# An FFT and maxout kernel on one core: stage one of the later batches in two groups of three, the single row by itself, and four edits at the two ends

## The chip, the core and the metric

The kernel runs on one core of a Trainium2 chip. A core has five engines with instruction streams of their own: TensorE (PE) multiplies matrices, with the loading of weights shown apart (PEld); VectorE (DVE), ScalarE (ACT) and GpSimd (POOL) do elementwise work; SyncE (SP) issues DMA transfers, as POOL and ACT can too. Engines wait for each other through semaphores. The metric is the device time of one execution in microseconds. Of the kernel before, the median of 3 runs is 388.24 us (387.73 to 388.91).

## The reference

```python
X = np.fft.fft(x, axis=1)            # x: (8, 3072, 256) float32
X = np.fft.fft(X, axis=2)
x = X.real.reshape(24576, 256)
h = np.maximum(np.maximum(x @ w1, x @ w2), x @ w3)   # w1, w2, w3: 256 x 768
out = h @ w_out                      # w_out: 768 x 256, out (24576, 256) float32
```

The Fourier transform runs over the sequence and over the channels, of which the real part is kept. Each of the 24576 rows then goes through three products, of which the largest is kept element by element, and an output layer.

## The kernel before

The transforms are matrix products with tables of cosines and sines. Over the sequence they are done in two stages. **Stage one** (`Mix.s`, from L386) multiplies the rows of one batch, held in `xt` as 49 rows of 256 columns with a mirrored copy in the lower half of the partitions, by a table `tab` of 64 columns. `s(0)` to `s(5)` take eight rows each with two matmuls side by side: `tile_position` (0, 0) and (0, 64) put the two products into the two halves of a PSUM bank. `s(6)` takes the single row 48, 64 output partitions by 128 columns (L404). ACT (in batch 1 DVE for some) copies each bank to `tb`. The result is transposed: in batch 0 on DVE, in later batches by a trip through DRAM, out with `y(0)`, `y(1)` and back with `z(0)`, `z(1)`, all issued by SP. **Stage two** (`Mix.k`) multiplies by the long tables and yields `tE` and `tO`, an even and an odd part over the first 1536 positions of the sequence. Even plus odd gives a row, even minus odd its mirrored row, so that half of the positions suffice.

The FFN of one batch is cut into 18 **units**: 3 blocks of 512 tokens by 6 chunks of 128 of the 768 hidden columns. The channel transform is folded into the weights (`g_all`, `gd_all`). Every unit yields `hp` for the plus rows and `hm` for the mirrored ones, and comes in two kinds:

- unsplit: `unit_plus` with four full matmuls (128x128 weights, 512 columns), ACT's `stmp` (L497) and DVE's maximum (L498) for `hp`; then `unit_minus` with two more matmuls, `stmp` and maximum again for `hm`. Six matmuls.
- split: `third(g)` computes the third product's even and odd part (two matmuls, L856 and L858), which ACT (`odd`, L860) and DVE (`even`, L861) bring to SBUF and POOL adds and subtracts (`plus` and `minus`, L865). `begin(g)` adds two matmuls (L875, L876) and one DVE operation (L877, `hp`), `finish(g)` one matmul (L491) and one DVE operation (L889, `hm`). Five matmuls, and two operations of POOL.

All odd units from unit 7 of batch 0 on are split; of the even ones those that `EXTRA` and `EXTRA_LAST` list: none in batch 0, units 0, 4, 8, 12 and 14 in the others. The output layer (`l2_block` and `l2_last`, matmuls L547, L563, L570) of each block is spread over the units of the next one.

The order on every engine is written out by hand: nothing is rearranged by a scheduler. The main loop walks over all 8 x 18 units: it begins unit g, finishes the unit before (where that one is split and g is not, it is finished first), computes the third product of unit g+2, issues scattering stores of mirrored rows at some units, then up to ten steps of the output layer, and then what `plan` holds for this unit: pieces of the next batch's stages (`ahead0` for batch 1, `ahead` for batches 2 to 7), loads of x (`load_x`, at units 13 and 18 of three batches before), and the mirror copies (`turn` and `mirror_first`). These copies are on ACT in eight parts, from units 5 to 12 of the batch two ahead of the one that they serve (3 units later for batch 2). 

PSUM banks: `ps_f` has three, shared in turn by stage one and two, the third products' `e3` and `d3`, and `pl`; `ps_s`, `ps_l1`, `ps_w3` and `ps_o` hold the head's products, the units' and the output layer's. In `ahead`, stage one of a later batch is in units 1 to 3: `s0`, `s1`; `s2`, `y0`, `s3`, `s6`; `s4`, `s5`, `y1`, `u` (`u` copies column 0 for a correction).

The head runs before the main loop: loads, the tables, batch 0's mirror copies in four parts (`FIRST`), stage one of batch 0 with some warming-up matmuls between, the transpose on DVE (L427), `k_first` for stage two of the first block (L696, evicted to `tE` and `tO` at L698), and the folded weights (L311 to L341, `gd_all` at L332). The mirror copies of batch 0 take column 0 separately (L133): on ACT, and on POOL for the parts from row 40 on.

Of the kernel before, what the change touches and what calls it, by code (L numbers as in the profile page):

```python
# [9 lines left out]
FP32 = mybir.dt.float32  # L10
# [4 lines left out]
ALU = mybir.AluOpType  # L15
# [13 lines left out]

FIRST_OF = (4, 8, 1)  # L30
PACE = (0, 4, 8, 14)
EXTRA, EXTRA_LAST = (0, 4, 8, 12, 14), (0, 4, 8, 12, 14)


def _parts(g):

    done = [(12 + i - 1, slice(128 * i + 96, 128 * i + 128)) for i in range(4)]
    for i in range(4 if g < 2 else 3):
        done.append((FIRST_OF[g] + i - 1, slice(128 * i, 128 * i + 96)))
    if g == 2:  # L40
        done += [(16, slice(384, 480, 2)), (15, slice(385, 480, 2))]
    return done
# [3 lines left out]
def kernel(  # L46
# [9 lines left out]
    nc = tc.nc  # L56

    B, S, D = x.shape
# [3 lines left out]
    TOKB = 512  # L62
    NHALF = 1536
    UNITS = 3 * NJC
# [8 lines left out]
    ps_f = ctx.enter_context(tc.tile_pool(name="ps_f", bufs=3, space=bass.MemoryType.PSUM))  # L73
# [30 lines left out]
    g_all = consts.tile([128, 4 * DFF], BF16, tag="g_all")  # L104
    g_all = g_all.rearrange("p (c k j) -> p c k j", k=4, j=128)
# [6 lines left out]
    sgn = consts.tile([128, 1], FP32, tag="sgn")  # L112
    wcol = consts.tile([128, NJC], FP32, tag="wcol")
    dif = consts.tile([128, 1], FP32, tag="dif")
# [9 lines left out]
    def mirror(b, s0, s1):  # L124

        t = xt[b % 2]
        fn = (nc.vector.tensor_copy, (nc.gpsimd.tensor_copy, nc.vector.tensor_copy)[s0 >= 25],
              nc.scalar.copy)[min(b, 2)]
        fn(out=t[64:128, s0:s1, 1:128], in_=t[0:64, s0:s1, 255:128:-1])  # L129
        if b < 2:  # L130
            if b == 0:
                fn = nc.scalar.copy if s0 < 40 else nc.gpsimd.tensor_copy
            fn(out=t[64:128, s0:s1, 0], in_=t[0:64, s0:s1, 128])  # L133

    def mirror_first(b):

        t = xt[b % 2]
        nc.scalar.copy(out=t[64:128, :, 0], in_=t[0:64, :, 128])
# [3 lines left out]
    ps_s = ps_s_cm.__enter__()  # L142
# [7 lines left out]
    pidx = gen.tile([128, 1], FP32, tag="pidx")  # L150
# [56 lines left out]
    turn = gen.tile([128, 2], FP32, tag="turn")  # L207
# [127 lines left out]
    def prep_first():  # L335

        for i in range(2):
            for half in range(2):
                psg = ps_f.tile([128, 512], FP32, name="psg", tag="ps")
                product(psg, 0, i, half, 384, 768)  # L340
                (nc.vector.tensor_copy, nc.scalar.copy)[half](  # L341
                    out=g_all[:, 3:6, 2 * i + half, :],
                    in_=psg[:, 0:384].rearrange("p (c j) -> p c j", j=128))
                if half:
                    differ(i, i + 1, 384, 768)
                yield
# [34 lines left out]
    class Mix:  # L381
# [8 lines left out]
        def s(self, k, pool=ps_f, evict=nc.scalar.copy):  # L390
            ps1 = pool.tile([128, 512], FP32, name="ps1", tag="ps")
            if k < 6:
                for hh in range(2):
                    nc.tensor.matmul(ps1[hh * 64:hh * 64 + 64], tab,  # L394
                                     self.x[:, 8 * k + hh:8 * k + 8:2, 0:128],
                                     start=True, stop=True, tile_position=(0, 64 * hh))
                if self.b:
                    evict(out=tbv[:, 4 * k:4 * k + 4, :],
                          in_=ps1.rearrange("p (s f) -> p s f", s=4))
                else:  # L400
                    evict(out=tbt[:, :, 4 * k:4 * k + 4, :],
                          in_=ps1.rearrange("p (s f l) -> p f s l", s=4, l=2))
            else:
                nc.tensor.matmul(ps1[0:64, 0:128], tab, self.x[:, 48, 0:128],  # L404
                                 start=True, stop=True, tile_position=(0, 0))
                if self.b:
                    evict(out=tbv[0:64, 24, :], in_=ps1[0:64, 0:128])
                else:
                    evict(out=tbt[0:64, :, 24, :],
                          in_=ps1[0:64, 0:128].rearrange("p (f l) -> p f l", l=2))  # L410
# [65 lines left out]
                                 tab[:, NHALF:NHALF + 1], start=True, stop=True)  # L476
            nc.scalar.copy(out=t_mid[:, :, self.b], in_=ps3[:, 0:2])

    def unit_plus(te, to, jc, n, pool3, tag3):

        pse2 = ps_l1.tile([128, TOKB], FP32, name="pse2", tag="pse2")
        pse3 = pool3.tile([128, TOKB], FP32, name="pse3", tag=tag3)
        for (pse, i) in ((pse2, 0), (pse3, 1)):
            nc.tensor.matmul(pse[:, 0:n], g_all[:, jc, 2 * i, :], te, start=True, stop=False)  # L484
            nc.tensor.matmul(pse[:, 0:n], g_all[:, jc, 2 * i + 1, :], to, start=False, stop=True)  # L485
        return pse2, pse3

    def unit_minus(pses, to, jc):
# [177 lines left out]
    def warm_up(n):  # L666
        for _ in range(n):
            nc.tensor.matmul(warm, zero[:, 0:128], zero, start=True, stop=True)
# [10 lines left out]
    m.s(2, pool=ps_s)  # L679
    m.s(3, pool=ps_s)  # L680
    warm_up(1)
    mirror(0, *FIRST[3])
    m.s(4, pool=ps_s)
    warm_up(2)
# [4 lines left out]
    def k_first(which):  # L689

        for h in range(2):
            ps2 = ps_s.tile([128, 512], FP32, name="ps2", tag="ps")
            for (i, cols) in _parts(0):
                at = cols.start - 256 * h
                if 0 <= at < 256:
                    nc.tensor.matmul(ps2[:, at:at + cols.stop - cols.start], m.col(i, which),  # L696
                                     (te_tab, to_tab)[which][:, cols], start=True, stop=True)
            (dve, nc.scalar.copy)[h](out=(m.tE, m.tO)[which][:, 256 * h:256 * h + 256],  # L698
                                     in_=ps2[:, 0:256])

    m.s(6, pool=ps_s)
    m.t()
    scal(sgn, pidx, 0.0, ALU.is_equal)
    scal(sgn, sgn, 2.0, ALU.mult, -1.0, ALU.add)
    scal(dif, sgn, 1.0, ALU.subtract)
    warm_up(2)
    nc.scalar.activation(out=nmd_all, in_=vm, func=AX.Sin, scale=float(-2.0 * math.pi / 256.0),
                         bias=turn[:, 1:2])
# [46 lines left out]
    ps_w3 = ctx.enter_context(tc.tile_pool(name="ps_w3", bufs=1, space=bass.MemoryType.PSUM))  # L755
    ps_o = ctx.enter_context(tc.tile_pool(name="ps_o", bufs=2, space=bass.MemoryType.PSUM))
# [3 lines left out]
    first, second = prep_first(), prep_second()  # L760
# [10 lines left out]
    def at(b, unit, fn):  # L771
        plan.setdefault((b + unit // UNITS, unit % UNITS), []).append(fn)
# [27 lines left out]
    def turn(b, ch):  # L800
        mirror(b, *EIGHTHS[ch])
# [16 lines left out]
    for b in range(2, B):  # L818
        for h in range(2):
            if b > 2:  # L820
                at(b - 3, (13, 18)[h], lambda b=b, h=h: load_x(b, 0, NS, h))
        for ch in range(8):
            at(b - 2, 5 + ch + 3 * (b == 2), lambda b=b, ch=ch: turn(b, ch))
        at(b - 2, 13 + 3 * (b == 2), lambda b=b: mirror_first(b))

    ahead0 = {3: ("s0", "s1"), 4: ("s2", "y0"), 5: ("s3", "s4"), 6: ("s5", "s6", "y1", "u"),
              7: ("z0", "z1"), 12: ("x",), 13: ("kO0",), 14: ("v0", "kE0", "kO1"),
              15: ("v1", "kE1"), 16: ("kO2",), 17: ("v2", "kE2", "end")}
    ahead = {1: ("s0", "s1"), 2: ("s2", "y0", "s3", "s6"), 3: ("s4", "s5", "y1", "u"),
             5: ("z0", "z1"), 11: ("x",), 12: ("kO0",), 13: ("v0", "kE0", "kO1"),  # L830
             14: ("v1", "kE1"), 15: ("kO2",), 16: ("v2", "kE2", "end")}
    for b in range(B - 1):
# [5 lines left out]

    def is_split(g):
        if g % 2 == 0:  # L840
            return (UNITS <= g < B * UNITS and
                    g % UNITS in (EXTRA if g < (B - 1) * UNITS else EXTRA_LAST))
        return 7 <= g < B * UNITS

    def operands(g):
# [21 lines left out]
    def begin(g, dst):  # L867

        te, to, _, jc = operands(g)
        if is_split(g):  # L870
            if g % 2:
                pse2 = ps_l1.tile([128, TOKB], FP32, name="pse2", tag="pse2")
            else:
                pse2 = ps_w3.tile([128, TOKB], FP32, name="pse3", tag="pse3")
            nc.tensor.matmul(pse2, g_all[:, jc, 0, :], te, start=True, stop=False)  # L875
            nc.tensor.matmul(pse2, g_all[:, jc, 1, :], to, start=False, stop=True)  # L876
            nc.vector.scalar_tensor_tensor(out=dst, in0=pse2, scalar=0.0, in1=sums[g][0],  # L877
                                           op0=ALU.max, op1=ALU.max)
            return (pse2,)
        pses = unit_plus(te, to, jc, TOKB, *((ps_o, "po") if g % 2 else (ps_w3, "pse3")))  # L880
        unit_out(pses, dst, TOKB)
        return pses

# [11 lines left out]
    for g in range(B * UNITS):  # L895
        b, u = divmod(g, UNITS)
        blk, jc = divmod(u, NJC)
# [68 lines left out]
```

## Time and profile before

| | |
|---|---|
| median of 3 runs | 388.24 us |
| profiled execution | 388.26 us |
| its span, first to last instruction | 386.5 us |
| granted TensorE clock | 1.00 |
| PE busy | 369.5 us, 96% |
| DVE, POOL, ACT busy | 87%, 86%, 63% |

Rows of the timeline give the start in microseconds from the start of the span, the duration (of several alike, from the first start to the last end), the engine, the line of the code (L12), the operation, output and inputs by the program's names with their sizes, the count (x2), and in brackets the idle time of the engine just before and what ended it. For a matmul the weights' shape comes first: 128*128 is a full one, 128*64 one that uses half of the array's columns. Matmuls overlap, so what one costs is read from one start to the next; their ends are modelled, and some of their records are missing from the trace. Rows of the windows give the window, its length, and the busy time (and count) of PE, PEld, DVE, ACT and POOL, the granted clock, the DMA engines' share and GB/s. Lines of the page are busy time, share and count of each engine.

### The profile page before, as it was taken

What the parts mean: (1) busy time and instruction counts of PE and PEld (TensorE: products, weight loads), DVE (VectorE), ACT (ScalarE), POOL (GpSimd) and SP (SyncE); (2) the same over time, 40 slices, a digit from 0 to 9 for tenths busy, and PEclk for the clock granted to TensorE, in tenths of its full rate; (3) what the DMA queues carried; (4) which work ended last, traced back from release to release, by engine and by line L of the source; (5) the groups of instructions that cost most, each with busy time, mean ns of one, the idle gap of its engine ahead of it and who ended that gap; (6) DMA issues with size and microseconds to landing.
All of it is one profiled execution on the core that took longest, in us unless ns stands there. A gap on an engine that the chain in (4) does not pass through costs nothing.

```text
span 386.5 us, 7957 instructions
## 1 busy us (share of the span) xinstructions
PE 369.5 (96%) x2737; PEld 234.8 (61%) x2786; DVE 335.7 (87%) x566; ACT 242.7 (63%) x455; POOL 331.7 (86%) x355
## 2 busy tenths in 40 slices
PE   6699999999999999999999999999999999999994
PEld 2354566565665666656665666666665667666664
DVE  7798797789997998989987998989987998989982
ACT  6877789567756677567756777567856436434320
POOL 9994557968999899989999899989988899879991
PEclk9999999999999999999999999999999999999999
DMA  8999736695269735695269834695224633312217
GB/s 118 168 197 152 158 114 101 189 162 177 71 133 204 196 120 106 181 213 180 67 120 200 209 110 112 188 187 184 85 56 128 186 113 97 96 61 98 77 63 225
DMA packets 51299, 54.13 MB, mean 140 GB/s; under 512 B 25813, under 2 KB 44268, under 8 KB 50563
## 3 DMA queue, kind: packets, MB, share of 16 engines
q0 software_dynamic: 19392, 26.45, 33.3%
q1 hardware_dynamic: 31334, 26.57, 26.5%
q10 hardware_dynamic: 532, 0.59, 0.5%
q8 instruction: 22, 0.36, 0.4%
q14 instruction: 19, 0.16, 0.1%
HBM read 36.95 MB, written 30.81 MB: 175 GB/s over the span
## 4 chain that ended last, share of the span: by engine, by line
PE 81%; POOL 9%; DVE 4%; issue 3%; ACT 2%; DVEq 0%; POOLq 0%
PE po L547 29%; PE pse L491 9%; PE pse L876 5%; PE e L856 5%; PE d L858 5%; PE pse L875 5%; PE po L570 4%; PE pse L485 4%; PE pse L484 3%; PE ps L460 3%; POOL plus L865 3%; PE ps L394 3%; PE pl L563 2%; POOL minus L865 2%; POOL xt L122 1%
## 5 line engine op out<-in xcount | busy, mean ns | idle before, releaser
L865 POOL TENSOR_TENSOR plus<-even,odd 128x512 bf16<-128x512 f32 x104 | 132.0, 1269 | 38.5 <-DVE even L861 31.1
L865 POOL TENSOR_TENSOR minus<-even,odd 128x512 bf16<-128x512 f32 x104 | 132.1, 1270 | 0.0
L860 ACT ACTIVATE odd<-d 128x512 f32<-128x512 f32 x104 | 62.1, 597 | 63.8 <-PE d L858 50.3
L877 DVE SCALAR_TENSOR_TENSOR hp<-pse,plus 128x512 bf16<-128x512 f32 x104 | 71.4, 687 | 26.0 <-PE pse L876 21.5
L547 PE MATMUL po<-wout_bf,hp 128*128 128x256 bf16 x576 | 86.1, 273 | 0.0
L547 PE MATMUL po<-wout_bf,hm 128*128 128x256 bf16 x576 | 78.6, 273 | 0.0
L861 DVE SCALAR_TENSOR_TENSOR even<-vb,wcol,e 128x512 f32<-128x512 bf16 x104 | 76.6, 737 | 0.0
L547 PEld LDWEIGHTS <-hp 128*128 128x128 bf16 x576 | 56.3, 98 | 26.2
L889 DVE SCALAR_TENSOR_TENSOR hm<-pse,minus 128x512 bf16<-128x512 f32 x104 | 70.7, 680 | 0.8 <-PE pse L485 0.4
L547 PEld LDWEIGHTS <-hm 128*128 128x128 bf16 x576 | 56.3, 98 | 16.3
L491 PE MATMUL pse<-tO,gd_all 128*128 128x512 bf16 x183 | 63.2, 380 | 0.8 <-DVE hp L877 0.2
L497 ACT ACTIVATE stmp<-pse 128x512 bf16<-128x512 f32 x80 | 47.5, 599 | 19.0 <-PE pse L491 8.8
L129 ACT COPY xt<-xt 64x762 bf16<-64x762 bf16 (+1 forms) x48 | 39.8, 838 | 2.3 <-DMA xt<-in_x_dram 1.3
L575 DVE TENSOR_TENSOR kq<-po,even 128x512 f32<-128x512 f32 x60 | 40.9, 682 | 0.0
L856 PE MATMUL e<-tE,g_all 128*128 128x512 bf16 x104 | 39.4, 379 | 0.3
L858 PE MATMUL d<-tO,gd_all 128*128 128x512 bf16 x104 | 39.4, 379 | 0.0
L876 PE MATMUL pse<-tO,g_all 128*128 128x512 bf16 x94 | 35.6, 379 | 1.7 <-issue 1.0
L570 PE MATMUL po<-gw,tO 128*128 128x512 bf16 x92 | 34.9, 379 | 0.0
L498 DVE TENSOR_TENSOR hp<-pse,stmp 128x512 bf16<-128x512 f32 x40 | 27.5, 687 | 6.7 <-ACT stmp L497 3.6
L875 PE MATMUL pse<-tE,g_all 128*128 128x512 bf16 x84 | 31.9, 380 | 0.7 <-DVE hm L498 0.5
L567 ACT COPY even<-pl 128x512 f32<-128x512 f32 x46 | 26.8, 583 | 8.3 <-DVE kq L575 7.8
L498 DVE TENSOR_TENSOR hm<-pse,stmp 128x512 bf16<-128x512 f32 x40 | 27.5, 687 | 4.2 <-ACT stmp L497 3.0
(183 smaller groups left out, 485.4 us busy)
## 6 DMA issues: line engine op xcount, KB each, us to landing
db<-tb SPq DMA_DIRECT2D x21, 192.0 KB
xt<-in_x_dram POOLq DMA_DIRECT2D x5, 784.0 KB, 8.2
xt<-in_x_dram POOLq DMA_DIRECT2D x5, 752.0 KB, 8.7
out_dram<-obuf SPq DMA_DIRECT2D x8, 384.0 KB
out_dram<-kq SPq DMA_DIRECT2D x8, 384.0 KB
vb<-vd SPq DMA_DIRECT2D x23, 128.0 KB
out_dram<-kq SPq DMA_DIRECT2D x7, 288.0 KB
out_dram<-kq SPq DMA_DIRECT2D x15, 128.0 KB
```

What stands on the lines that cost most here:

```text
L491: nc.tensor.matmul(pse, gd_all[:, jc, i, :], to, start=False, stop=True, skip_group_check=True)
L498: nc.vector.tensor_tensor(out=dst, in0=src3, in1=stmp[:, 0:n], op=ALU.max)
L547: nc.tensor.matmul(po, hcols(jc), wout_bf[:, jc * 256:(jc + 1) * 256], start=False, stop=(jc == NJC - 1), skip_group_check=True)
L856: nc.tensor.matmul(e3, g_all[:, jc, 2, :], te, start=True, stop=True)
L858: nc.tensor.matmul(d3, gd_all[:, jc, 1, :], to, start=True, stop=True)
L860: nc.scalar.activation(out=odd3, in_=d3, func=AX.Copy, scale=-0.5)
L861: nc.vector.scalar_tensor_tensor(out=even3, in0=vb, scalar=wcol[:, jc:jc + 1], in1=e3, op0=ALU.mult, op1=ALU.add)
L865: nc.gpsimd.tensor_tensor(out=dst, in0=even3, in1=odd3, op=op)
L875: nc.tensor.matmul(pse2, g_all[:, jc, 0, :], te, start=True, stop=False)
L876: nc.tensor.matmul(pse2, g_all[:, jc, 1, :], to, start=False, stop=True)
L877: nc.vector.scalar_tensor_tensor(out=dst, in0=pse2, scalar=0.0, in1=sums[g][0], op0=ALU.max, op1=ALU.max)
L889: nc.vector.scalar_tensor_tensor(out=dst, in0=pses[0], scalar=0.0, in1=sums.pop(g)[1], op0=ALU.max, op1=ALU.max)
```

## The change

Five things change.

1. In `ahead`, the pieces of stage one of batches 2 to 7 stand in units 1 to 3 as `s0`, `s1`, `s2`, `y0`; `s3`, `s4`, `s5`; `s6`, `y1`, `u`. The matmul of the single row loses its `tile_position`.
2. Units 12 and 14 of batch 0 are split, and unit 14 of the last batch is not.
3. Batch 3's mirror copies, `turn` and `mirror_first`, come one unit later.
4. In the head, column 0 of the parts from row 40 on is copied by DVE; the three one-column operations on `sgn` and `dif` move ahead of a mirror copy; `k_first(1)` takes its banks from `ps_f`.
5. Unit 0 runs its four matmuls as even, even, odd, odd.

```diff
-EXTRA, EXTRA_LAST = (0, 4, 8, 12, 14), (0, 4, 8, 12, 14)
+EXTRA = (12, 14), (0, 4, 8, 12, 14), (0, 4, 8, 12)
...
             if b == 0:
-                fn = nc.scalar.copy if s0 < 40 else nc.gpsimd.tensor_copy
+                fn = nc.scalar.copy if s0 < 40 else nc.vector.tensor_copy
             fn(out=t[64:128, s0:s1, 0], in_=t[0:64, s0:s1, 128])
...
                 nc.tensor.matmul(ps1[0:64, 0:128], tab, self.x[:, 48, 0:128],
-                                 start=True, stop=True, tile_position=(0, 0))
+                                 start=True, stop=True)
...
-        for (pse, i) in ((pse2, 0), (pse3, 1)):
-            nc.tensor.matmul(pse[:, 0:n], g_all[:, jc, 2 * i, :], te, start=True, stop=False)
-            nc.tensor.matmul(pse[:, 0:n], g_all[:, jc, 2 * i + 1, :], to, start=False, stop=True)
+        steps = [(pse2, 0, 0), (pse2, 0, 1), (pse3, 1, 0), (pse3, 1, 1)]
+        if first:
+            steps = steps[0::2] + steps[1::2]
+        for (pse, i, k) in steps:
+            nc.tensor.matmul(pse[:, 0:n], g_all[:, jc, 2 * i + k, :], (te, to)[k],
+                             start=(k == 0), stop=(k == 1))
...
     m.s(3, pool=ps_s)
     warm_up(1)
+    scal(sgn, pidx, 0.0, ALU.is_equal)
+    scal(sgn, sgn, 2.0, ALU.mult, -1.0, ALU.add)
+    scal(dif, sgn, 1.0, ALU.subtract)
     mirror(0, *FIRST[3])
...
-            ps2 = ps_s.tile([128, 512], FP32, name="ps2", tag="ps")
+            ps2 = (ps_s, ps_f)[which].tile([128, 512], FP32, name="ps2", tag="ps")
...
     m.t()
-    scal(sgn, pidx, 0.0, ALU.is_equal)
-    scal(sgn, sgn, 2.0, ALU.mult, -1.0, ALU.add)
-    scal(dif, sgn, 1.0, ALU.subtract)
     warm_up(2)
...
-            at(b - 2, 5 + ch + 3 * (b == 2), lambda b=b, ch=ch: turn(b, ch))
-        at(b - 2, 13 + 3 * (b == 2), lambda b=b: mirror_first(b))
+            at(b - 2, 5 + ch + 3 * (b == 2) + (b == 3), lambda b=b, ch=ch: turn(b, ch))
+        at(b - 2, 13 + 3 * (b == 2) + (b == 3), lambda b=b: mirror_first(b))
...
-    ahead = {1: ("s0", "s1"), 2: ("s2", "y0", "s3", "s6"), 3: ("s4", "s5", "y1", "u"),
+    ahead = {1: ("s0", "s1", "s2", "y0"), 2: ("s3", "s4", "s5"), 3: ("s6", "y1", "u"),
...
-            return (UNITS <= g < B * UNITS and
-                    g % UNITS in (EXTRA if g < (B - 1) * UNITS else EXTRA_LAST))
+            return g < B * UNITS and g % UNITS in EXTRA[(g >= UNITS) + (g >= (B - 1) * UNITS)]
...
-        pses = unit_plus(te, to, jc, TOKB, *((ps_o, "po") if g % 2 else (ps_w3, "pse3")))
+        pses = unit_plus(te, to, jc, TOKB, *((ps_o, "po") if g % 2 else (ps_w3, "pse3")),
+                         first=(g == 0))
```

More of the change, by code (lines that the diff above doesn't have):

```diff
@@ L477, in end, with unit_plus @@
             nc.scalar.copy(out=t_mid[:, :, self.b], in_=ps3[:, 0:2])
-    def unit_plus(te, to, jc, n, pool3, tag3):
+    def unit_plus(te, to, jc, n, pool3, tag3, first=False):
         pse2 = ps_l1.tile([128, TOKB], FP32, name="pse2", tag="pse2")
         pse3 = pool3.tile([128, TOKB], FP32, name="pse3", tag=tag3)
-        for (pse, i) in ((pse2, 0), (pse3, 1)):
-            nc.tensor.matmul(pse[:, 0:n], g_all[:, jc, 2 * i, :], te, start=True, stop=False)
-            nc.tensor.matmul(pse[:, 0:n], g_all[:, jc, 2 * i + 1, :], to, start=False, stop=True)
+        steps = [(pse2, 0, 0), (pse2, 0, 1), (pse3, 1, 0), (pse3, 1, 1)]
[4 more added lines that the diff above has]
+                             start=(k == 0), stop=(k == 1))
         return pse2, pse3
```

## The prediction

> **What bounds the kernel now.** I read the busy shares of the page first, then a window in the middle, then the timeline at each place the change touches.
>
> ```profile
> span 386.5 us, 7957 instructions
> PE 369.5 (96%) x2737; PEld 234.8 (61%) x2786; DVE 335.7 (87%) x566; ACT 242.7 (63%) x455; POOL 331.7 (86%) x355
> ...
> 100.00:150.00 50.00, 49.47 (x390) 32.33 (x397) 44.88 (x71) 34.78 (x64) 46.80 (x44) 1.00 0.61 148
> ```
>
> PE is busy for 369.5 of 386.5 us, and for 49.47 of the 50 us from 100 to 150, at the full clock (the 1.00). In the middle of the kernel a microsecond is won only by taking work or stalls from PE, and another engine's delay costs nothing until PE waits for it. DVE (44.88) and POOL (46.80) leave little room, so such a delay is near. The profiled execution took 388.26 us, the span plus 1.8 outside it, and the median of the runs is 388.24, so I subtract from 388.26.
>
> **Part 1: the groups of stage one.** Batch 3's, in the timeline:
>
> ```profile
> 161.09 0.74 DVE L861 SCALAR_TENSOR_TENSOR even<-vb,wcol,e 128x512 f32<-128x512 bf16 x1
> 161.14 0.38 PE L547 MATMUL po<-wout_bf,hp 128*128 128x256 bf16 x2
> 161.45 0.62 PE L394 MATMUL ps<-xt,tab 128*64 128x512 bf16 x4
> 161.90 1.07 ACT L398 CAST tb<-ps 128x512 bf16<-128x512 f32 x2 [0.75 <-issue]
> 162.00 0.39 PE L491 MATMUL pse<-tO,gd_all 128*128 128x512 bf16 x1
> 162.23 0.38 PE L484 MATMUL pse<-tE,g_all 128*128 128x512 bf16 x1
> 162.86 0.61 ACT L497 ACTIVATE stmp<-pse 128x512 bf16<-128x512 f32 x1
> 163.50 0.69 DVE L498 TENSOR_TENSOR hp<-pse,stmp 128x512 bf16<-128x512 f32 x1 [0.31 <-PE e L856]
> 163.96 0.82 PE L547 MATMUL po<-wout_bf,hm 128*128 128x256 bf16 x6
> 164.11 0.74 DVE L861 SCALAR_TENSOR_TENSOR even<-vb,wcol,e 128x512 f32<-128x512 bf16 x1
> 164.71 0.62 PE L394 MATMUL ps<-xt,tab 128*64 128x512 bf16 x4
> 165.16 0.22 PE L404 MATMUL ps<-xt,tab 128*64 128x128 bf16 x1
> 165.54 0.38 PE L876 MATMUL pse<-tO,g_all 128*128 128x512 bf16 x1 [0.16 <-issue]
> ...
> 341.58 0.82 PE L547 MATMUL po<-wout_bf,hp 128*128 128x256 bf16 x6
> ...
> 342.55 0.82 PE L547 MATMUL pom<-wout_bf,hmid 128*8 128x256 bf16 x6
> 343.30 0.39 PE L875 MATMUL pse<-tE,g_all 128*128 128x512 bf16 x1
> ```
>
> Full matmuls follow each other every 0.22 (162.00 to 162.23), 256-column ones every 0.11. Two of these from 161.14 end at 161.36, but the first s matmul starts at 161.45: 0.09 to enter the 128*64 form. Each pair (two matmuls side by side) takes 0.24, so the second starts at 161.69 and would release PE at 161.91; the next full matmul starts at 162.00, 0.09 more. The group thus takes 0.64, the 0.48 of its pairs and two switches. The group with the single row s6 runs from 164.61 (163.96 plus six times 0.11) to 165.32 (165.54 less one L875 whose record is missing), 0.71. Before, a batch has 0.64 + 0.71 + 0.64 = 1.99 (2.01 unrounded).
>
> After, it has two groups of three pairs, 0.64 + 0.24 = 0.88 each, and s6 alone. Is that "common matmul" common? L404 reads 128*64: the form follows the table's 64 columns, and dropping the argument changes nothing in the built instruction. The nearest row without the argument is the middle row's 128*8 matmul: six L547 from 341.58 end at 342.23, and the six 128*8 ones from 342.55 would end at 343.20, but the next full matmul starts at 343.30, 0.10 later. Of the 0.71 above, the entry and two pairs are 0.57, and s6 with the way out 0.14 to 0.16. Alone it needs a way in too: 0.09 + 0.16 = 0.25. Sum 0.88 + 0.88 + 0.25 = 2.01, +0.02 a batch and +0.1 over six. Were s6 free of switches, it would cost 0.06 (a 128-column step, a quarter of 0.22) and the batch 1.82, less by 0.18. Ends: -1.1 and +0.1; I take +0.1, by L404's own form.
>
> The Trainium skill (page "TensorEngine Tiling (Array Packing)", section "Key Properties") says that changing the tiling mode makes the array drain. The 0.09 on each side agrees; by that rule as by the rows, a lone s6 pays a drain for itself, and the sum stays.
>
> A group of three delays what the other engines queue behind it. The third pair's eviction holds ACT for 0.48 more (two casts take 1.07), so stmp goes from 162.86 to 163.34, hp from 163.50 to 163.98, even from 164.11 to 164.59, ending at 165.33. Its PSUM bank is what the next group needs: its third pair would start at 164.71 + 0.24 + 0.48 = 165.43, against 165.33 and the 0.05 a release takes. The first group's third pair needs the bank of even at 161.09 (161.83 + 0.05 = 161.88), and is due at 161.93. Both margins are 0.05. SP's order of transfers stays; y0 goes out a unit earlier and y1 0.6 earlier, neither awaited before unit 5. I charge no stall. Ends: 0, and the whole 0.48 in one or both groups (first rival).
>
> **Part 2: the head.**
>
> ```profile
> 13.36 0.65 DVE L129 COPY xt<-xt 64x1143 bf16<-64x1143 bf16 x1 [0.84 <-DMA xt<-in_x_dram]
> ...
> 14.04 0.22 POOL L133 COPY xt<-xt 64x9 bf16<-64x9 bf16 x1
> 14.31 0.41 PE L394 MATMUL ps<-xt,tab 128*64 128x512 bf16 x2 [0.74 <-POOL xt L133]
> ...
> 19.86 0.37 ACT L698 CAST tE<-ps 128x256 bf16<-128x256 f32 x1 [0.19 <-PE ps L696]
> ...
> 20.62 0.38 PE L484 MATMUL pse<-tE,g_all 128*128 128x512 bf16 x1 [0.46 <-ACT tO L698]
> ...
> 25.67 1.56 POOL L129 COPY xt<-xt 64x1651 bf16<-64x1651 bf16 x1
> ...
> 25.93 1.44 DVE L332 TENSOR_SCALAR gd_all<-g_all,dif 128x384 bf16<-128x384 bf16 x1 [0.17 <-ACT g_all L341]
> ...
> 29.29 0.35 DVE L332 TENSOR_SCALAR gd_all<-g_all,dif 128x384 bf16<-128x384 bf16 x1 [0.26 <-ACT g_all L341]
> ...
> 34.49 0.18 DVE L133 COPY xt<-xt 64x12 bf16<-64x12 bf16 x1
> ```
>
> PE waits at 14.31 for POOL's small copy (L133), itself behind DVE's mirror copy ending at 14.01. On DVE the copy takes 0.18 (34.49) and overlaps the end of the copy ahead, so it should end near 14.12 and PE start at 14.17: -0.14, kept through the transpose that follows on DVE. The three one-column operations moved ahead go into DVE's 0.84 of idle before 13.36; uncovered they would cost about 0.5. Unit 0's first matmul waits for tO at 20.62 (idle 0.46); with the two even matmuls first it waits for tE only, ready at 19.86 + 0.37 = 20.23, less the 0.14: 20.14 against 20.62. The head as a whole gives -0.48. The spare bank for k_first only removes a wait; I give it nothing. Ends: -0.56 and -0.14 (second rival).
>
> **Part 3: units 12 and 14 of batch 0 split.** A unit unsplit has six full matmuls, split five: -2 x 0.216 = -0.43. Each split unit adds a plus and a minus on POOL.
>
> ```profile
> 58.09 1.27 POOL L865 TENSOR_TENSOR plus<-even,odd 128x512 bf16<-128x512 f32 x1 [2.14 <-ACT xt L129]
> ...
> 72.91 0.62 PE L394 MATMUL ps<-xt,tab 128*64 128x512 bf16 x4
> ...
> 84.82 0.82 ACT L129 COPY xt<-xt 64x762 bf16<-64x762 bf16 x1 [1.32 <-DMA xt<-in_x_dram]
> ...
> 89.48 0.38 PE L875 MATMUL pse<-tE,g_all 128*128 128x512 bf16 x1 [0.54 <-DVE hm L498]
> ...
> 117.60 0.62 PE L394 MATMUL ps<-xt,tab 128*64 128x512 bf16 x4
> ```
>
> Two pairs of 1.27 are 5.1 on POOL, in a stretch where it idles 2.14 ahead of a single plus; the rest can push back batch 2's copies and the x load issued from POOL. I give it no cost; the other end is in the fourth rival.
>
> **Part 4: batch 3's copies a unit later.** First groups of stage one start at 72.91, 117.60 and 161.45: batch 1 takes 44.69, batch 2 43.85, so batch 1 has 0.84 to lose. ACT's first copy waits 1.32 for the x load until 84.82, its own work then queues, and PE waits down to 89.48 (0.54 there). A unit is 43.85 / 18 = 2.4 us, more than the 1.32, so the wait goes; ACT's following work, bunched by a unit elsewhere, is late next, for 0.14: -0.70. Ends: 0 and -0.84. POOL's L865 covers the later mirror_first as before.
>
> **Part 5: the last batch's unit 14 unsplit.**
>
> ```profile
> 368.68 0.82 PE L547 MATMUL po<-wout_bf,hp 128*128 128x256 bf16 x6
> ...
> 369.01 0.69 DVE L877 SCALAR_TENSOR_TENSOR hp<-pse,plus 128x512 bf16<-128x512 f32 x1 [1.16 <-POOL plus L865]
> ...
> 369.75 0.38 PE L491 MATMUL pse<-tO,gd_all 128*128 128x512 bf16 x1 [0.25 <-DVE hp L877]
> ...
> 372.20 0.38 PE L875 MATMUL pse<-tE,g_all 128*128 128x512 bf16 x1
> ```
>
> Between 368.68 and 372.20 PE issues fourteen 256-column matmuls (six L547 with hp, six with hm, two with hp), and six full ones (five of the units, one L570): 14 x 0.109 + 6 x 0.216 = 2.82 of 3.52. The 0.70 is waiting that begins with POOL's late plus (idle 1.16). Without unit 14's pair POOL is 2.5 earlier, and the wait goes; one more full matmul costs 0.216; ACT and DVE take back the unsplit unit's stmp and max, under PE's work while DVE has the idle seen here. -0.70 + 0.22 = -0.48. Ends: -0.48 and +0.22.
>
> **Sum.** +0.1 - 0.48 - 0.43 - 0.70 - 0.48 = -1.99: 388.26 - 1.99 = 386.3.
>
> **The rivals.**
> Slower: three pairs in a group stall PE. ACT's 0.48, with margins of 0.05 in both groups, would become PE time; the place is the second group's third pair. From 1.97 / 6 = 0.33 a batch the gain is gone, and from 0.52 the kernel is slower by 0.3% (1.16 us, about what a measurement can tell from no change). One group stalling 0.48 gives 386.3 + 2.9 = 389.2, both 392.1. Against it: the chain above comes out at 0.05 to spare twice. For it: that is the reading error of two rows.
> Head gain lost: DVE's L332 took 1.44 at 25.93 while POOL's copy ran from 25.67, and 0.35 at 29.29 without it. If the earlier start lets POOL in first, only 0.14 of 0.48 remains: 386.65. The Trainium skill (page "SBUF — State Buffer", section "🔬 SBUF: two separate sides") calls the pair of ports that these engines share an exclusive lock, kept for a whole instruction by whichever starts first. The 1.44, ending 0.14 after POOL's copy does, agrees.
> s6 does become common: six times 0.18 less, 386.3 - 1.2 = 385.1. For it only the code's words; against it L404's form.
> Batch 3's copies still wait: the load comes later by POOL's extra work, and the 0.70 is lost: 387.0.
> Several parts give half: about 387.3, within 0.3%.
>
> **How the numbers follow.** Forecast 0.50, slower rival 0.10 (0.03 of it within 0.3%), head lost 0.12, s6 common 0.08, copies waiting 0.12 (half beyond 0.3%, whose bound is 387.1), halves 0.08. Faster 0.50 + 0.12 + 0.08 + 0.06 = 0.76; same 0.06 + 0.08 + 0.03 = 0.17; slower 0.07. The range 385.3 to 387.6 leaves out s6 common with the rest and the stalls, some 0.18.
>
> **What would show it.** Groups in after: 0.88 between the matmuls on either side of six L394 (before +3 lines), and s6 alone at 0.25, read as 128*64; no idle before either third pair. Head: PE's first unit at 20.1. Batch 1: from group to group under 44.1. Around unit 15 of the last batch: no wait of DVE for POOL. The prediction is wrong if idle before a stage-one matmul repeats in every batch, or if POOL's loads in batch 0 arrive later than ACT's copies.

## The result and the profile after

The changed kernel has a median of 386.50 us (14 runs, 385.51 to 387.91) against 387.81 us (14 runs) of the kernel before beside it. The ratio is 0.9962 with a 95% interval of 0.9950 to 0.9974, so about 1.5 us less (1.0 to 1.9): a gain of 0.4%, small but with its whole interval below 1. Its profiled execution took 386.44 us, 1.82 less than the 388.26 before. The forecast was 386.3, a gain of 1.97 against the profiled execution (1.99 in the prediction's sum, which rounds the groups' six times 0.02 to 0.1).

The page after, and the window from 100 to 150 us (length, busy time and count of PE, PEld, DVE, ACT, POOL, granted clock, DMA share, GB/s):

```profile
span 384.6 us, 8010 instructions
PE 372.9 (97%) x2785; PEld 235.9 (61%) x2785; DVE 336.6 (88%) x568; ACT 242.3 (63%) x454; POOL 333.7 (87%) x356
...
100.00:150.00 50.00, 50.00 (x391) 32.25 (x389) 44.33 (x71) 34.99 (x64) 46.39 (x45) 1.00 0.61 145
```

PE seems to have more busy time in a shorter span. That is a matter of records: this trace holds 48 more PE matmuls, where the one before had lost some. Busy sums can't be compared here, and starts of the same instruction can. Five rows cut the kernel into its stages. Of the kernel before, the prediction shows those at 20.62, 72.91 and 117.60, and the other two are:

```profile
292.99 0.41 PE L394 MATMUL ps<-xt,tab 128*64 128x512 bf16 x2
...
380.77 0.82 PE L547 MATMUL po<-wout_bf,hm 128*128 128x256 bf16 x6
```

Of the changed kernel (lines from L484 on have moved by up to 6):

```profile
20.44 0.59 PE L487 MATMUL pse<-tE,g_all 128*128 128x512 bf16 x2
...
72.29 0.41 PE L394 MATMUL ps<-xt,tab 128*64 128x512 bf16 x2
...
116.18 0.41 PE L394 MATMUL ps<-xt,tab 128*64 128x512 bf16 x2
...
291.72 0.62 PE L394 MATMUL ps<-xt,tab 128*64 128x512 bf16 x4
...
379.06 0.82 PE L550 MATMUL po<-wout_bf,hm 128*128 128x256 bf16 x6
```

In each kernel these are unit 0's first matmul, the first group of the stage one that runs in batch 1, in batch 2 and in batch 6, and PE's last group.

| stage | before | after | difference | forecast for it |
|---|---|---|---|---|
| head, to unit 0 | 20.62 | 20.44 | -0.18 | -0.48 |
| unit 0 to the first group in batch 1 | 52.29 | 51.85 | -0.44 | -0.43 |
| batch 1, group to group | 44.69 | 43.89 | -0.80 | -0.70, +0.02 for its groups |
| batches 2 to 5, each (a quarter of 117.60 to 292.99, or of 116.18 to 291.72) | 43.85 | 43.885 | +0.04 | +0.02 |
| batch 6's group to PE's last group | 87.78 | 87.34 | -0.44 | -0.48, +0.02 for its groups |
| PE's last group to the end of the span | 5.7 | 5.5 | -0.2 | 0 |

On PE that is -0.18 - 0.44 - 0.80 + 0.15 - 0.44 = -1.7 us. The last line is the output's stores; between the kernels below, which share that tail, the same stretch came out between 5.1 and 5.8, so its 0.2 is no gain that could be put down to an edit.

The groups of stage one in batch 3, after:

```profile
159.76 0.38 PE L550 MATMUL po<-wout_bf,hp 128*128 128x256 bf16 x2
160.07 0.85 PE L394 MATMUL ps<-xt,tab 128*64 128x512 bf16 x6
160.85 0.39 PE L494 MATMUL pse<-tO,gd_all 128*128 128x512 bf16 x1
...
166.09 0.82 PE L550 MATMUL po<-wout_bf,hp 128*128 128x256 bf16 x6
166.84 0.24 PE L404 MATMUL ps<-xt,tab 128*64 128x128 bf16 x1
167.02 0.39 PE L877 MATMUL pse<-tE,g_all 128*128 128x512 bf16 x1
```

Two matmuls of 0.11 end at 159.98, and PE goes on with full matmuls at 160.85: 0.87 for three pairs. The single row is a 128*64 matmul as before, without the argument too. Its neighbours' work ends at 166.09 + 6 x 0.109 = 166.75, and the next full matmul starts at 167.02, so the row takes 0.27 by itself. The second group, by the same reckoning, takes 0.89 (163.46 to 164.35). No row has an idle mark: no stall is seen.

### The profile page after: what moved, and what is told of

Its sections match the earlier page's. It is cut to its first block, busy times and chain, and to the rows that moved or that the text cites. A ratio compares the mean times of both kernels' runs of the same rounds, so it can differ in the third digit from the quotient of the medians.

```text
span 384.6 us, 8010 instructions
## 1 busy us (share of the span) xinstructions
PE 372.9 (97%) x2785; PEld 235.9 (61%) x2785; DVE 336.6 (88%) x568; ACT 242.3 (63%) x454; POOL 333.7 (87%) x356
## 4 chain that ended last, share of the span: by engine, by line
PE 90%; DVE 3%; ACT 3%; issue 1%; POOL 1%; POOLq 0%; DVEq 0%; ACTq 0%
PE po L550 32%; PE pse L494 10%; PE pse L487 8%; PE pse L877 6%; PE pse L878 6%; PE e L858 6%; PE d L860 6%; PE po L573 5%; PE ps L460 3%; PE ps L394 3%; PE pl L566 3%; DVE yb L427 1%; ACT stmp L500 1%; PE psg L311 1%; POOL xt L122 1%
## 5 line engine op out<-in xcount | busy, mean ns | idle before, releaser
L862 ACT ACTIVATE odd<-d 128x512 f32<-128x512 f32 x105 | 62.9, 599 | 62.5 <-PE d L860 34.8
L863 DVE SCALAR_TENSOR_TENSOR even<-vb,wcol,e 128x512 f32<-128x512 bf16 x105 | 77.4, 737 | 0.0
L500 ACT ACTIVATE stmp<-pse 128x512 bf16<-128x512 f32 x78 | 46.6, 602 | 21.4 <-PE pse L487 10.3
L877 PE MATMUL pse<-tE,g_all 128*128 128x512 bf16 x105 | 39.9, 380 | 0.1
L878 PE MATMUL pse<-tO,g_all 128*128 128x512 bf16 x105 | 39.8, 379 | 0.0
L501 DVE TENSOR_TENSOR hp<-pse,stmp 128x512 bf16<-128x512 f32 x39 | 26.7, 686 | 6.9 <-ACT stmp L500 5.6
```

What stands on the lines that cost most here:

```text
L862: nc.scalar.activation(out=odd3, in_=d3, func=AX.Copy, scale=-0.5)
L863: nc.vector.scalar_tensor_tensor(out=even3, in0=vb, scalar=wcol[:, jc:jc + 1], in1=e3, op0=ALU.mult, op1=ALU.add)
```

## Experiments

All but three of these kernels were executed once, and the profile is read at the stage that the edit touches. The head's position moves by up to 2 us between executions with the landing of the first loads, so a single time says little, and lengths between two rows of the same trace are compared.

### The groups alone

```diff
 # the kernel before
-                                 start=True, stop=True, tile_position=(0, 0))
+                                 start=True, stop=True)
...
-    ahead = {1: ("s0", "s1"), 2: ("s2", "y0", "s3", "s6"), 3: ("s4", "s5", "y1", "u"),
+    ahead = {1: ("s0", "s1", "s2", "y0"), 2: ("s3", "s4", "s5"), 3: ("s6", "y1", "u"),
```

> The kernel before with the regrouping alone: stage one of batches 2 to 7 in two groups of three pairs, the single row by itself. My theory: the groups take what the changed kernel's trace shows, 0.87 and 0.90 us, and the single row 0.27 with a switch on each side, 2.04 a batch against 2.01 before; six batches give +0.2 us, so the time is 0.1 to 0.3 us above the kernel before, inside its noise. Rival: the regrouping is what made the changed kernel faster (fewer switches), and this kernel alone is 1.0 us or more below the kernel before. Second rival: without the other edits the third pairs find their banks occupied, and PE stalls by up to 0.48 a group, +2.9 to +5.8 us.

Ratio 1.0013 (0.9997 to 1.0030): no difference that can be told, and surely no gain of 1 us. Batches 2 to 5 take 43.89 each, 0.04 more than before, as in the changed kernel. The rival of fewer switches falls, and so does that of stalls. But batch 1 came out shorter than expected:

```profile
72.92 0.84 PE L394 MATMUL ps<-xt,tab 128*64 128x512 bf16 x6
...
84.03 0.82 ACT L129 COPY xt<-xt 64x762 bf16<-64x762 bf16 x1 [0.47 <-DMA xt<-in_x_dram]
...
117.00 0.84 PE L394 MATMUL ps<-xt,tab 128*64 128x512 bf16 x6
```

It takes 44.08 instead of 44.69, although batch 3's copies were not shifted. ACT's first copy waits 0.47 for the load instead of 1.32. The 0.19 above the other batches is not this wait's: the third and fourth copy end at 90.17, and ACT then idles 2.07, which takes up any delay before it.

### The shift alone, and the changed kernel without it

```diff
 # the kernel before, shift added
-            at(b - 2, 5 + ch + 3 * (b == 2), lambda b=b, ch=ch: turn(b, ch))
-        at(b - 2, 13 + 3 * (b == 2), lambda b=b: mirror_first(b))
+            at(b - 2, 5 + ch + 3 * (b == 2) + (b == 3), lambda b=b, ch=ch: turn(b, ch))
+        at(b - 2, 13 + 3 * (b == 2) + (b == 3), lambda b=b: mirror_first(b))
```

> The kernel before with the shift of batch 3's mirror copies alone. My theory: ACT's first copy comes after the load has landed, and batch 1 takes 43.85 to 44.0 us instead of 44.69: 0.7 to 0.85 less. Rival: the wait only moves to other copies or to the work that ACT has bunched into the next unit, and batch 1 stays above 44.3.

```profile
73.81 0.41 PE L394 MATMUL ps<-xt,tab 128*64 128x512 bf16 x2
...
87.51 0.82 ACT L129 COPY xt<-xt 64x762 bf16<-64x762 bf16 x1
...
117.67 0.62 PE L394 MATMUL ps<-xt,tab 128*64 128x512 bf16 x4
```

43.86: the excess goes, to within 0.01 of the other batches' 43.85, and ACT's copy waits for nothing. The opposite edit, the same two lines as before in the changed kernel:

> The changed kernel with batch 3's mirror copies back in their earlier units. Read from first group of batch 2's stage one to first group of batch 3's (batch 1's length): 44.69 us in the kernel before, 43.89 in the changed one. My theory as predicted: the shift of the copies took the whole excess, so without it ACT waits 1.3 us for the load and batch 1 takes 44.7 again. Rival, from the kernel with the regrouping alone, where batch 1 took 44.08 although the copies were not shifted: the regrouping, which sends stage one's first transfer out 2 us earlier, lets the load land 0.8 us earlier and took most of the excess; then batch 1 takes 44.05 to 44.15 here and ACT waits some 0.5 us.

```profile
72.56 0.84 PE L394 MATMUL ps<-xt,tab 128*64 128x512 bf16 x6
...
83.81 0.83 ACT L129 COPY xt<-xt 64x762 bf16<-64x762 bf16 x1 [0.62 <-DMA xt<-in_x_dram]
...
116.44 0.84 PE L394 MATMUL ps<-xt,tab 128*64 128x512 bf16 x6
```

43.88, the length of the changed kernel: without the shift nothing was lost in this execution, though ACT waited 0.62. My theory for this kernel falls, and the rival named the right side but 0.2 too long. From the x load's issue (72.82 before, 72.84 with the groups alone, 72.47 here) to the copy that waited for it, it takes 12.0, 11.2 and 11.3 us, and stage one's first transfer leaves 2 to 3 us earlier with the groups (SP issues it at 77.23 before, at 74.96 and at 74.59). That looks as if the groups made the load land sooner. The landing of the same load in all the traces says otherwise. The view of its issue (`--source L122`, from 70 to 76 us) of the kernel before, of the groups alone, and of the changed kernel:

```profile
DMA to landing us min/median/max: 11.9/11.9/11.9
...
DMA to landing us min/median/max: 11.1/11.1/11.1
...
DMA to landing us min/median/max: 13.0/13.0/13.0
```

With the old groups it takes 11.9 and, with the shift alone, 11.5. With the new ones, over the changed kernel and the eleven others on this page that have them, it takes 10.1 to 13.2, above 12 in six of the twelve. The changed kernel and the four below that differ from it in the head alone have 13.0, and 12.8, 13.2, 10.6 and 11.0, so what sets it is not the groups, and no run shows what it is. The groups alone and this kernel were executed with an early landing. An unshifted copy is ready 10.7 after the issue (84.82 - 1.32 - 72.82) and waits or not as the landing falls; the shifted one starts 13.6 to 14.0 after it in every trace that has the shift, behind every landing seen, and batch 1 then takes what the other batches of its kernel take. So the shift is the cure that is shown. That the groups cure the stall too is not shown, and the timed runs of the groups alone have no gain.

### The ends of the kernel

```diff
 # the changed kernel
-EXTRA = (12, 14), (0, 4, 8, 12, 14), (0, 4, 8, 12)
+EXTRA = (), (0, 4, 8, 12, 14), (0, 4, 8, 12, 14)
```

> The changed kernel with the even units of batch 0 and of the last batch as before (none split in batch 0; unit 14 of the last batch split). My theory: from unit 0's first matmul to the first group of batch 2's stage one 52.28 us instead of 51.86 (two matmuls of 0.216 more), and from the last batch's stage one to the end of PE 88.36 instead of 87.88 (POOL late again, three waits of 0.7 less one matmul of 0.216): +0.43 and +0.48. Rival: the copies and the load in batch 0 take part of its gain, so that undoing it costs less than 0.3.

```profile
22.29 0.59 PE L487 MATMUL pse<-tE,g_all 128*128 128x512 bf16 x2
...
74.58 0.62 PE L394 MATMUL ps<-xt,tab 128*64 128x512 bf16 x4
...
294.00 0.62 PE L394 MATMUL ps<-xt,tab 128*64 128x512 bf16 x4
...
370.04 0.69 DVE L879 SCALAR_TENSOR_TENSOR hp<-pse,plus 128x512 bf16<-128x512 f32 x1 [1.17 <-POOL plus L867]
...
381.81 0.82 PE L550 MATMUL po<-wout_bf,hm 128*128 128x256 bf16 x6
```

Unit 0 to batch 1 takes 52.29 again, 0.44 more, and the last stretch 87.81, 0.47 more, with DVE's 1.17 of waiting for POOL back. Both terms stand. (The head ran late here by 1.9 us, which is before the first row.)

### The single row without its switches

```diff
 # the changed kernel
-    tab = consts.tile([128, 64], BF16, tag="tab")
+    tab = consts.tile([128, 128], BF16, tag="tab")
...
+    nc.gpsimd.memset(tab[:, 64:128], 0.0)
...
-                    nc.tensor.matmul(ps1[hh * 64:hh * 64 + 64], tab,
+                    nc.tensor.matmul(ps1[hh * 64:hh * 64 + 64], tab[:, 0:64],
...
-                nc.tensor.matmul(ps1[0:64, 0:128], tab, self.x[:, 48, 0:128],
+                w = 128 if self.b > 1 else 64
+                nc.tensor.matmul(ps1[0:w, 0:128], tab[:, 0:w], self.x[:, 48, 0:128],
```

> The changed kernel, but the table of stage one is padded with 64 columns of zeros for the single row of batches 2 to 7, so that its matmul has 128 weight columns like its neighbours. My theory: what the single row costs by itself is the two switches of the array, 0.09 in and 0.12 out beside 0.06 of its own; padded it takes 0.06, so each of six batches gets shorter by 0.21 us, 1.3 us in all: 385.2 against 386.5. Rival: the 0.27 is a wait for its PSUM bank or its operands, and the padded row pays it too: no change, 386.5.

```profile
166.23 0.82 PE L552 MATMUL po<-wout_bf,hp 128*128 128x256 bf16 x6
166.88 0.22 PE L406 MATMUL ps<-xt,tab 128*128 128x128 bf16 x1
166.97 0.38 PE L879 MATMUL pse<-tE,g_all 128*128 128x512 bf16 x1
```

Ratio to the kernel before 0.9918 (0.9904 to 0.9933), median 385.37. The row is now 128*128 and takes 0.09 (166.97 less 166.23 + 0.65) instead of 0.27, and batches 2 to 5 take 43.70 instead of 43.885 (116.50 to 291.30, a quarter). Over six batches 1.1 us, where I had written 1.3: next to full matmuls the row costs 0.09, not the 0.06 of a 128-column step. So 0.18 of the 0.27 was the change of form and nothing else, and this kernel is faster than both (each timed beside the kernel before): its interval lies wholly below the changed kernel's 0.9950 to 0.9974.

### How much room a group of three pairs has

```diff
 # the changed kernel, the row behind the second group
-    ahead = {1: ("s0", "s1", "s2", "y0"), 2: ("s3", "s4", "s5"), 3: ("s6", "y1", "u"),
+    ahead = {1: ("s0", "s1", "s2", "y0"), 2: ("s3", "s4", "s5", "s6"), 3: ("y1", "u"),
```

> The changed kernel with the single row right behind the second group's three pairs, a fourth bank in one go. My theory (the rival on stalls, priced from the changed kernel's rows of batch 3): the row needs the first of the three banks, which ACT has cleared at 164.59 + 0.05, where it would start at 164.25: PE waits 0.4; the switch saved gives back 0.2, so each batch gets longer by 0.1 to 0.3 us, six batches 0.6 to 1.8. Rival: no wait, and each batch gets shorter by 0.2.

```profile
163.87 0.87 PE L394 MATMUL ps<-xt,tab 128*64 128x512 bf16 x6
164.95 0.22 PE L404 MATMUL ps<-xt,tab 128*64 128x128 bf16 x1 [0.21 <-ACT tb L398]
165.10 0.39 PE L877 MATMUL pse<-tE,g_all 128*128 128x512 bf16 x1
```

Batches 2 to 5 take 44.04, 0.15 more than in the changed kernel. The row starts 1.08 after the group where three pairs would let it start at about 0.68: the wait of 0.4 for the first bank, as worked out; the switch that is saved gives the rest back.

```diff
 # the changed kernel, the two small copies on ACT between two evictions
+    ahead = {1: ("s0", "s1", "s2", "y0"), 2: ("s3", "u", "s4", "s5"), 3: ("s6", "y1"),
```

> The changed kernel with the two small copies for the correction (0.27 and 0.19 us on ACT, 0.36 from start to start) between the first and the second eviction of the second group, so that the banks of the second and third pair come free 0.36 later. My theory (the margins of about 0.05 that the prediction worked out are real): the third product's second matmul waits 0.04 and the output layer's first matmul about 0.3 for the third pair's bank, so batches 2 to 6 take about 44.2 us instead of 43.89. Rival: there is more room than that, or other waits absorb it, and the batches stay at 43.9 to 43.95.

```profile
165.98 1.08 ACT L398 CAST tb<-ps 128x512 bf16<-128x512 f32 x2
...
166.67 0.38 PE L860 MATMUL d<-tO,gd_all 128*128 128x512 bf16 x1
...
167.11 0.38 PE L566 MATMUL pl<-gw,tE 128*128 128x256 bf16 x2
```

The two evictions end at 167.06, and `pl`, which needs the last one's bank, starts at 167.11 and not 0.216 after 166.67, at 166.89: a wait of 0.22, with the 0.05 of a release behind it. Batches take 44.10, 0.21 more. An eviction only 0.27 later thus reaches PE with 0.22 (in the changed kernel the last one starts 0.96 after the first, here 1.23): the room of `pl` was about 0.05. The two margins that the prediction worked out are others, those of the third pairs, and the changed kernel's own trace has them. DVE's `even` before the second group in batch 3 ends at 163.22 + 0.74 = 163.96 and frees its bank 0.05 later, at 164.01; the third pair is due at 163.55 + 0.24 + 0.22 = 164.01 and starts then. Before the first group `even` ends at 160.46, and the third pair starts at 160.53, 0.02 after its bank is free. The other batches have the same, to 0.01.

### The head

Three edits of it, undone one at a time, and a fourth that takes POOL's loading of the weights out of the way.

```diff
 # the changed kernel, column 0 on POOL again
-                fn = nc.scalar.copy if s0 < 40 else nc.vector.tensor_copy
+                fn = nc.scalar.copy if s0 < 40 else nc.gpsimd.tensor_copy
```

> The changed kernel with column 0 of batch 0's last part copied on POOL again. My theory: in the changed kernel DVE's copy of that column takes 0.47 us and the mirror copy before it 0.78, because POOL writes transfer descriptors beside them; back on POOL, that work is held back behind the copy, the mirror copy takes 0.65 again and the head's matmul group starts 0.15 to 0.3 us earlier than 14.46, as does all after it: end of PE 0.15 to 0.3 earlier. Rival: the three one-column operations moved ahead push the mirror copy and are what costs; then PE still starts at 14.4 or later.

```profile
14.34 0.41 PE L394 MATMUL ps<-xt,tab 128*64 128x512 bf16 x2 [0.80 <-POOL xt L133]
```

PE's group started at 14.34, 0.12 earlier than in the changed kernel and where the kernel before has it (14.31). So in these two executions DVE's copy had cost and not gained. The mirror copy before it took no less (0.96), which was wrong in my theory.

```diff
 # the changed kernel, POOL's second load of the weights behind the two copies
-    for k in range(3):
-        load_w(k, 384, 768)
     m.u()
+    for k in range(3):
+        load_w(k, 384, 768)
```

> The changed kernel with POOL's second load of the weights issued after the two copies for the correction instead of before, so that POOL writes no descriptors while DVE copies. My theory (POOL's descriptor work slows DVE's copies): the mirror copy takes 0.65 and the column copy 0.18 to 0.22 on DVE, PE's group starts near 14.05 to 14.15 instead of 14.46, 0.3 to 0.4 us earlier to the end. Rival: the column copy is slow on DVE in itself: it still takes 0.47 and PE starts at 14.35 or later.

This head ran late by 0.7 with its loads, but DVE's column copy took 0.17 instead of 0.47, and PE started 0.76 after the mirror copy's start (13.93 to 14.69) instead of 1.24 (13.22 to 14.46). Later this kernel lost that again: PE waited 0.81 for POOL's copy (at 31.32), which had itself waited 1.74 for batch 1's load, and from unit 0 to the first group in batch 1 it took 52.28 instead of 51.85. POOL issues that load behind the weights'; but in the padded kernel, with the old order, it waited 1.03 there, so the order is not the only cause. The same with the padded table:

> The changed kernel with the padded table for the single row (as the padded kernel measured alone) and POOL's second load of the weights behind the two copies for the correction. My theory: six batches get shorter by 0.19 each, as measured there, 1.1 us in all, and the head by up to 0.3 more, as DVE's column copy takes 0.17 instead of 0.47: 0.989 to 0.992 of the kernel before. Rival: the load of the weights, later by 1.6 us, delays the folded weights, and the head's gain is gone: the time of the padded kernel or above, 0.992 to 0.994.

Ratio 0.9932 (0.9915 to 0.9948), median 385.56; the span of its profile, 383.0, is the shortest of the profiled ones. Its time lies in the rival's range, 0.992 to 0.994, and not in mine: a gain of the head is not to be seen beside the padded kernel alone, whose median is 385.37. From unit 0 to batch 1 it took 51.85, so the later load cost PE nothing in this execution. What the head gains up to unit 0 the traces show, since this head and the changed kernel's run alike up to 13.93. The changed kernel's:

```profile
13.22 0.78 DVE L129 COPY xt<-xt 64x1143 bf16<-64x1143 bf16 x1
13.93 0.47 DVE L133 COPY xt<-xt 64x9 bf16<-64x9 bf16 x1
...
13.62 2.21 POOL L184 DMA_DIRECT2D w_bf<-in_moe_w_dram  x3
...
14.46 0.41 PE L394 MATMUL ps<-xt,tab 128*64 128x512 bf16 x2 [0.77 <-DVE xt L133]
```

and with the load behind:

```profile
13.93 0.16 DVE L133 COPY xt<-xt 64x9 bf16<-64x9 bf16 x1
...
14.15 0.41 PE L395 MATMUL ps<-xt,tab 128*64 128x512 bf16 x2 [0.51 <-DVE xt L133]
...
20.11 0.59 PE L489 MATMUL pse<-tE,g_all 128*128 128x512 bf16 x2
```

The same copy of nine elements from the same instant takes 0.47 and 0.16, and PE starts at 14.15 and unit 0 at 20.11, where the prediction had 14.17 and 20.14. The three writings of the load take 2.21, about 0.74 each; the first, from 13.62, ends near 14.40, and the copy at 13.93 + 0.47 = 14.40. The writing need not come in the way, though. The padded kernel above, with the load in its old place, has

```profile
14.29 2.21 POOL L184 DMA_DIRECT2D w_bf<-in_moe_w_dram  x3
...
14.52 0.16 DVE L133 COPY xt<-xt 64x9 bf16<-64x9 bf16 x1
```

Of the eight traces with this copy on DVE and the load in its old place, six have a copy of 0.28 to 0.47 that starts 0.31 or more after the writing and ends within 0.01 of its end. This one starts 0.23 after it and takes 0.16; the eighth is the last kernel below. So a few tenths of a microsecond between the two decide whether the copy is held up.

```diff
 # the changed kernel, unit 0 in the old order
-        pses = unit_plus(..., first=(g == 0))
+        pses = unit_plus(..., first=False)
```

> The changed kernel with unit 0's four matmuls in the old order. My theory: the first odd matmul waits for tO with the first even one stuck in front of nothing useful; from the first table matmul of the first block to unit 0's second unit it takes 0.3 to 0.4 us more. Measured from the start of the first table matmul (19.54 in the changed kernel) to the start of stage one's group after unit 2 (29.88): 10.34 in the changed kernel, 10.68 in the kernel before (19.38 to 30.06), and 10.65 to 10.7 here. Rival: the order is worth nothing and the difference comes from the three one-column operations that were moved away from between: then 10.35 to 10.45.

```profile
19.76 0.44 PE L702 MATMUL ps<-te_tab,yb 128*128 128x32 bf16 x8 [0.84 <-DVE yb L427]
...
20.67 0.38 PE L487 MATMUL pse<-tE,g_all 128*128 128x512 bf16 x1
21.01 0.38 PE L487 MATMUL pse<-tO,g_all 128*128 128x512 bf16 x1
```

The first matmul starts 0.91 after the first table matmul, as in the changed kernel (0.90), and not 1.24 as before; only the second waits, 0.34 behind the first instead of 0.22. The stretch to stage one's group takes 10.48 (19.76 to 30.24), between the 10.34 and the 10.68. Neither side's numbers fit. The order is worth 0.14 and something else 0.2.

```diff
 # the changed kernel, the banks of k_first(1) as before
-            ps2 = (ps_s, ps_f)[which].tile([128, 512], FP32, name="ps2", tag="ps")
+            ps2 = ps_s.tile([128, 512], FP32, name="ps2", tag="ps")
```

> The changed kernel with the banks of k_first(1) in ps_s again, unit 0's new order kept. From the first table matmul of the first block to unit 0's first matmul it takes 0.90 us in the changed kernel, 0.91 with unit 0's old order and 1.24 in the kernel before. My theory, formed on the run with the old order: unit 0's banks lie where those of k_first(1) lay, so its first matmul waited for tO's eviction whatever its operands; with the banks back it waits again, 1.2 to 1.25, and the order alone is worth nothing. Rival: moving the three one-column operations away took that wait, and 0.90 stays.

```profile
13.79 0.17 DVE L133 COPY xt<-xt 64x9 bf16<-64x9 bf16 x1
...
13.97 2.16 POOL L184 DMA_DIRECT2D w_bf<-in_moe_w_dram  x3
...
19.07 0.45 PE L702 MATMUL ps<-te_tab,yb 128*128 128x32 bf16 x8 [0.60 <-DVE yb L427]
...
20.32 0.59 PE L487 MATMUL pse<-tE,g_all 128*128 128x512 bf16 x2 [0.46 <-ACT tO L704]
```

1.25 from the table to unit 0, with the wait for `tO` as before: the new order alone is worth nothing, and neither are the three operations moved away (19.07 to 29.76 is 10.69, against 10.68 before). The bank, with these operations moved, gives 0.2, and bank and order together 0.34. This run also shows the copy on DVE with the load in its old place, but this time POOL's first writing starts 0.01 after the copy's end: the copy takes 0.17.

## Why the prediction was right, and where it was not

The direction, the size (1.97 forecast, 1.7 on PE, about 1.5 by the ratio of the timed runs, 1.3 between their medians) and the range hold. Term by term:

**Groups, +0.1: right in kind, at half of what came.** It was 0.04 a batch, 0.2 over six. The single row alone costs 0.27 where 0.25 was charged, and the groups 0.87 and 0.89 where 0.88 was. That the argument's removal does nothing, by the row's own 128*64 form, was the point on which a rival of -1.2 hung; the padded table shows that this rival described a real gain of 1.1, which this change does not make. The Trainium skill (page "TensorEngine Tiling (Array Packing)", section "Key Properties") speaks of a drain at a change of tiling mode; the padded row, 0.09 instead of 0.27, agrees.

**The room of 0.05: right, and nearer still.** The margins came out at 0.02 and at nothing. The slower rival did not happen, but it stood as near as worked out: with evictions later by less than 0.3 `pl` waits 0.22, and a fourth bank in the group costs 0.4 of waiting.

**Batch 0's units and the last batch, -0.43 and -0.48: right**, each shown by its undoing (+0.44, +0.47).

**Batch 3's copies, -0.70: the step is right, the size is one execution's.** -0.84 went between the two profiles; the 0.14 set aside for ACT's bunched work was not needed. The step took the 1.32 of waiting as the kernel's. It was one execution's: the load takes 10.1 to 13.2 us to land, and without the shift batch 1 took 44.69, 44.08 and 43.88. A unit's shift, 2.4, was enough for all landings seen, with 0.4 to spare at the latest (13.2 against the copies' 13.6). How much the timed runs owe to it is not known.

**The head, -0.48: wrong, -0.18 came.** The failing step is "on DVE the copy takes 0.18": in the kernel before, POOL's copy held POOL's load of the weights back behind it, and moving the copy let that load start beside DVE. The copy took 0.47 and PE's group came 0.15 later instead of 0.14 earlier, in this execution and, by the copy's length, in five of the seven others alike. The prediction costed the copy on its new engine and not what its leaving set free on the old one. The row it needed was in the trace of before:

```profile
14.18 2.17 POOL L184 DMA_DIRECT2D w_bf<-in_moe_w_dram  x3
```

POOL goes on with the load right behind its copy, whose row starts at 14.04. The rival on DVE and POOL had the mechanism, but at another pair of instructions. By the Trainium skill (page "SBUF — State Buffer", section "🔬 SBUF: two separate sides") whichever of DVE, in a mode that uses both of its ports, and POOL starts first keeps the shared ports for its whole instruction. 0.47 ending with POOL's writing when POOL was first, and 0.17 when DVE was first, agree; 0.16 in the padded kernel, where POOL's row starts 0.23 ahead, does not agree by the recorded starts. No run shows in which mode the copy ran or which engine held the ports there, and POOL's recorded spans are rough. Unit 0's 0.34 is right as a sum, with a wrong share. "The spare bank for k_first only removes a wait; I give it nothing" is the step that fails: without the bank the new order gives nothing, and the bank gives 0.2 of the 0.34 even with the old order.

## What to carry to other kernels

When an operation leaves an engine, ask what stands behind it in that engine's queue: it starts earlier, and may run into the very work that was moved. A stall behind a load has the size that the load's landing has in that execution: look at the landing in several traces before a price is put on it, and before an edit that left it shorter is called its cure. And the form of this matmul followed its operands: a narrow one among full ones paid for the change of form, which zero columns in its weights avoided.

## What was unexpected of the hardware

A copy of nine elements on DVE took 0.28 to 0.47 instead of 0.16 to 0.17 us when POOL had begun to write a transfer's descriptors 0.31 us or more before it, and ended within 0.01 of that writing's end (six traces); with POOL's row only 0.23 ahead it took 0.16, and where the copy began first 0.17. One load, issued at the same place of the program, took from 10.1 to 13.2 us to land in fourteen traces. Padding a 64-column weight table to 128 made one small matmul cheaper, from 0.27 to 0.09 us.
